# Hedgehog attention and a squared-ReLU FFN: another order of the plan's steps from position 100 on, with its bank, engine, gate and warm-up tables

## The chip, the cores and the metric

The kernel runs on 1 core of one Trainium2 chip. The metric is the device time of one launch in microseconds, taken as the median of the runs. TensorE is called PE (its weight load PEld), VectorE DVE, ScalarE ACT, GpSimd POOL and SyncE SP, as in the profile.

## The reference

Linear attention with learned features over 8 batches, 8 heads, 576 tokens and 64 columns per head, then an FFN over the 4608 rows that the attention gives.

```python
def phi(x):
    proj = np.einsum('bhsd,df->bhsf', x, w_phi)
    proj = proj - np.max(np.abs(proj), axis=-1, keepdims=True)
    return np.concatenate([np.exp(proj), np.exp(-proj)], axis=-1)
q_p, k_p = (phi(q), phi(k))
kv = np.einsum('bhsf,bhsd->bhfd', k_p, v)
z = np.sum(k_p, axis=2)
num = np.einsum('bhsf,bhfd->bhsd', q_p, kv)
den = np.einsum('bhsf,bhf->bhs', q_p, z)[..., None] + 1e-06
x = (num / den).transpose(0, 2, 1, 3).reshape(4608, 512)
h = np.maximum(x @ w_in, 0.0)      # 512 -> 2048
out = h * h @ w_out                # 2048 -> 512
```

`w_phi` is 64x128, so each head has 256 features: exp(proj) and exp(-proj).

## The kernel before, in words

All products are bf16 with f32 sums in PSUM. The work is cut into 8 batches of attention and 9 FFN chunks of 512 tokens: chunk c (0 to 7) takes the first 512 tokens of batch c, and chunk 8 takes the last 64 tokens of each of the eight.

One batch of attention goes through these steps. q, k and v are loaded by POOL's DMA queue (`load`, L254 and L262; `load_q`, L274 and L285). q and k are transposed: from batch 2 on by a DMA transpose that SP issues (`transposed`, L339), before that on PE. PE projects them (L355, with 64 rows of the array; L510 and L577 in the first batch and for the features of q), DVE takes the largest absolute value (`em_ops` L410, `qmax_ops` L517, L389 in the first batch), ACT forms the exponentials (L416 and L398 for k, L592 for q). `v_ops` (L443) multiplies V by exp of its keys' maxima, which ACT wrote (L429, L435); the product stands on DVE or, in batches 0 and 1, on either DVE or POOL. `kv_ops` (L473, L478) sums keys by values in PSUM; ACT or DVE copies the sums to SBUF (L196 on DVE, L198 on ACT). `out_ops` multiplies with the features of q (L607), DVE scales (L619), takes the reciprocal of the denominator (L627) and divides (L631, into the tile xo). xo is transposed to xT (xS for chunk 8): by a DMA transpose on SP (L665), in the first batch on PE with a DVE copy (L656).

An FFN chunk has 16 groups of each kind: `ffn_in` (called F1 here, L751; `ffn_in_small` L762 for chunk 0, by pieces of 128 tokens) multiplies with w_in, `relu_sq` takes the ReLU (L726 on ACT, L728 on DVE, into hr) and the square (L735, on DVE, or in chunks 0 and 1 on either DVE or POOL); `ffn_out` (F2, L816) multiplies with w_out, ACT or DVE copies the sums out (L198, L196), and SP stores them (L832, L835). `last_out` ends chunk 8 by halves of 256 columns (product L780, copies L794 and L796, store L803). The weights are loaded by POOL (`load_win` L301, `load_wout` L307).

None of this is emitted where it is written. Each step is a closure that `Plan.add` records, 1731 in all, and five tables decide the rest. `arrange` (L101) returns the steps in the order of `ORDER`, gives each PSUM group its bank from `BASES`, and reads from `STATES` which of its two engines a step with alternatives takes:

```python
for op in self.ops:
    if op.alt is not None and STATES[op.group] == "1":
        op.eng, op.occ, op.lat = op.alt
for g, b in zip(self.banks, BASES):
    g.base = int(b)
return [self.ops[i] for i in ORDER]
```

`pin` (L139) chains every instruction to the one before it on its engine, so that an engine runs its share of the steps strictly in the order of the table. For the loads it adds a wait for one other step, taken from `GATES`; the last table, `FILL`, puts warm-up matmuls on PE ahead of some steps (L885), which compute nothing that is used:

```python
dep(i, before, mybir.DependencyClass.NoSync)
...
if now[0].seq in GATES:
    dep(i, plan.ops[GATES[now[0].seq]].ins, mybir.DependencyClass.Sync)
```

Of the kernel before, what the change touches and what calls it, by code (L numbers as in the profile page):

```python
# [111 lines left out]
def kernel(  # L112
# [783 lines left out]
    59, 80, 94, 92, 35, 83, 155, 61, 63, 95, 34, 74, 98, 49, 85, 169, 62, 104, 57, 93, 100, 25, 103, 60, 58, 101,  # L896
    158, 102, 84, 81, 99, 97, 127, 143, 105, 24, 82, 106, 96, 159, 107, 125, 28, 128, 108, 129, 126, 156, 160, 131,
    130, 170, 37, 219, 132, 213, 157, 121, 133, 214, 147, 134, 220, 172, 148, 135, 173, 117, 136, 149, 137, 118, 33,
    174, 150, 161, 151, 199, 36, 231, 200, 162, 183, 381, 197, 232, 184, 138, 163, 198, 215, 139, 164, 187, 140, 152,
    165, 188, 322, 216, 189, 374, 166, 323, 325, 185, 153, 217, 167, 154, 221, 168, 233, 222, 337, 326, 218, 38, 331,  # L900
    234, 223, 376, 334, 327, 332, 378, 338, 328, 224, 324, 225, 335, 329, 175, 379, 340, 235, 339, 330, 375, 343,
    171, 333, 236, 176, 352, 226, 341, 336, 344, 342, 177, 377, 190, 353, 178, 346, 179, 370, 186, 246, 191, 261,
    347, 286, 262, 180, 287, 192, 355, 30, 193, 288, 194, 207, 349, 208, 181, 209, 182, 264, 345, 195, 210, 356, 498,
    196, 211, 265, 502, 239, 350, 263, 245, 248, 227, 212, 277, 238, 367, 228, 237, 240, 278, 371, 358, 380, 242,
    229, 247, 372, 364, 244, 357, 254, 253, 230, 241, 39, 243, 506, 256, 373, 368, 255, 249, 32, 369, 257, 348, 250,
    31, 279, 251, 359, 361, 351, 266, 258, 389, 354, 259, 252, 365, 280, 362, 201, 281, 203, 260, 516, 204, 202, 282,
    267, 283, 295, 284, 520, 296, 268, 289, 510, 297, 290, 270, 360, 304, 271, 291, 305, 524, 511, 292, 528, 366,
    293, 269, 272, 306, 388, 298, 363, 307, 299, 552, 529, 308, 205, 300, 206, 577, 556, 301, 302, 386, 309, 313,
    273, 310, 572, 560, 314, 274, 311, 275, 316, 276, 294, 315, 534, 317, 437, 285, 468, 438, 564, 318, 512, 439,
    440, 469, 319, 303, 538, 441, 470, 571, 542, 312, 320, 570, 565, 390, 434, 391, 398, 567, 321, 546, 399, 392,  # L910
    387, 499, 393, 569, 435, 400, 503, 581, 547, 495, 401, 584, 504, 574, 394, 442, 413, 500, 496, 450, 521, 385,
    451, 505, 395, 568, 507, 522, 383, 452, 523, 517, 508, 382, 396, 406, 501, 384, 459, 518, 513, 397, 768, 519,
    585, 535, 497, 460, 514, 539, 536, 436, 515, 411, 461, 407, 531, 767, 540, 446, 402, 532, 415, 549, 573, 509,
    418, 447, 410, 408, 575, 525, 533, 537, 576, 409, 403, 557, 578, 412, 419, 550, 553, 416, 583, 421, 541, 543,
    579, 554, 420, 427, 582, 526, 443, 417, 695, 558, 530, 527, 775, 404, 551, 548, 414, 699, 764, 429, 405, 444,
    765, 424, 422, 771, 426, 425, 555, 544, 561, 766, 423, 545, 471, 428, 769, 562, 453, 703, 559, 580, 454, 477,
    472, 455, 478, 430, 563, 456, 473, 457, 707, 479, 474, 458, 475, 432, 431, 708, 587, 591, 433, 586, 599, 592,
    749, 753, 600, 593, 757, 588, 594, 713, 589, 462, 717, 590, 463, 566, 445, 601, 480, 476, 464, 481, 721, 602,
    465, 709, 466, 482, 725, 448, 609, 483, 467, 484, 486, 603, 487, 595, 604, 761, 485, 726, 780, 449, 488, 731,
    596, 961, 608, 605, 489, 776, 735, 762, 615, 616, 962, 606, 490, 739, 778, 618, 624, 597, 491, 972, 626, 743,  # L920
    610, 623, 492, 607, 970, 617, 598, 692, 493, 777, 744, 631, 625, 494, 640, 967, 693, 656, 704, 641, 657, 773,
    782, 700, 770, 612, 705, 611, 632, 658, 968, 718, 971, 701, 706, 634, 643, 722, 774, 644, 694, 969, 710, 614,
    723, 613, 702, 779, 696, 724, 719, 635, 963, 711, 619, 633, 781, 697, 647, 620, 637, 772, 665, 720, 714, 638,
    666, 965, 621, 966, 698, 667, 629, 715, 728, 646, 636, 639, 716, 648, 712, 674, 729, 740, 622, 642, 630, 730,
    649, 650, 746, 651, 741, 668, 675, 742, 652, 747, 736, 676, 964, 653, 669, 732, 654, 645, 737, 670, 758, 655,
    733, 671, 672, 627, 738, 759, 763, 734, 788, 683, 754, 789, 980, 750, 760, 790, 755, 928, 628, 791, 659, 932,
    660, 751, 756, 677, 684, 661, 892, 783, 662, 685, 678, 936, 748, 663, 679, 752, 896, 680, 681, 800, 796, 784,
    900, 785, 801, 727, 786, 904, 682, 787, 940, 797, 807, 802, 664, 910, 941, 803, 914, 905, 805, 804, 811, 821,
    906, 792, 793, 828, 820, 798, 799, 745, 673, 918, 922, 808, 794, 806, 946, 813, 795, 1162, 829, 950, 840, 831,
    844, 923, 809, 845, 815, 841, 954, 1167, 846, 812, 686, 832, 810, 889, 897, 979, 958, 890, 981, 687, 834, 973,  # L930
    823, 891, 1158, 982, 688, 898, 976, 924, 814, 822, 1164, 893, 833, 959, 983, 1159, 1160, 984, 689, 901, 902, 907,
    1166, 824, 975, 826, 835, 690, 903, 894, 837, 960, 825, 908, 827, 853, 691, 978, 854, 838, 1165, 862, 1170, 855,
    816, 915, 818, 895, 1161, 1163, 830, 856, 911, 899, 817, 916, 1001, 909, 933, 819, 857, 917, 1168, 836, 1004,
    858, 863, 912, 859, 839, 860, 977, 1174, 919, 847, 848, 864, 934, 974, 880, 951, 881, 920, 849, 882, 925, 850,
    935, 913, 929, 926, 952, 865, 843, 851, 937, 842, 930, 871, 866, 1025, 921, 938, 943, 867, 947, 927, 1026, 931,
    872, 939, 944, 852, 868, 1175, 873, 1003, 869, 948, 955, 1176, 861, 874, 997, 875, 956, 998, 1027, 1089, 876,
    877, 878, 1028, 1125, 999, 1129, 985, 1037, 1172, 957, 953, 1000, 1002, 986, 1093, 1097, 949, 987, 945, 988, 870,
    1169, 883, 1101, 1038, 884, 1039, 1042, 1133, 1102, 879, 993, 1040, 885, 994, 886, 1029, 1137, 1005, 1143, 1017,
    887, 1138, 989, 1049, 1094, 1050, 995, 996, 1147, 1095, 1051, 1096, 942, 1018, 1178, 990, 1179, 1086, 1054, 1008,
    1052, 1151, 1020, 1007, 1112, 1010, 1019, 1087, 1180, 991, 1113, 1009, 1006, 1171, 1098, 1090, 1103, 1041, 1155,  # L940
    1181, 992, 1061, 1011, 1099, 1012, 1091, 1156, 1062, 1100, 1073, 1021, 1053, 1023, 1015, 1013, 1063, 1024, 1114,
    1030, 1016, 1022, 1130, 1014, 1031, 1104, 1074, 1088, 1064, 1177, 1032, 1043, 1044, 1075, 1131, 1076, 1105, 1033,
    1116, 1055, 1045, 1122, 888, 1139, 1198, 1034, 1201, 1117, 1065, 1077, 1035, 1106, 1092, 1046, 1047, 1363, 1107,
    1056, 1182, 1194, 1364, 1361, 1057, 1195, 1365, 1111, 1356, 1359, 1115, 1058, 1357, 1059, 1119, 1183, 1196, 1123,
    1067, 1197, 1036, 1124, 1118, 1066, 1358, 1060, 1134, 1068, 1108, 1069, 1120, 1173, 1140, 1200, 1184, 1185, 1152,
    1109, 1070, 1222, 1370, 1366, 1135, 1202, 1071, 1141, 1110, 1078, 1360, 1136, 1223, 1190, 1186, 1079, 1126, 1048,
    1153, 1072, 1224, 1187, 1127, 1154, 1304, 1225, 1188, 1308, 1207, 1286, 1226, 1189, 1205, 1132, 1199, 1148, 1128,
    1295, 1142, 1290, 1191, 1192, 1149, 1355, 1150, 1080, 1203, 1291, 1193, 1081, 1206, 1372, 1294, 1292, 1082, 1144,
    1083, 1209, 1084, 1287, 1145, 1146, 1293, 1312, 1246, 1227, 1296, 1208, 1121, 1247, 1288, 1234, 1204, 1283, 1297,
    1316, 1309, 1298, 1284, 1317, 1248, 1212, 1235, 1322, 1310, 1299, 1236, 1373, 1249, 1313, 1300, 1311, 1213, 1327,  # L950
    1314, 1250, 1157, 1301, 1379, 1328, 1375, 1237, 1285, 1289, 1326, 1376, 1239, 1302, 1380, 1377, 1305, 1323, 1214,
    1362, 1306, 1307, 1303, 1331, 1216, 1378, 1330, 1324, 1341, 1215, 1270, 1238, 1381, 1315, 1382, 1325, 1258, 1334,
    1332, 1217, 1251, 1342, 1210, 1374, 1271, 1398, 1272, 1333, 1211, 1397, 1319, 1218, 1343, 1259, 1085, 1273, 1219,
# [80 lines left out]
```

## Time and profile before

| what | value |
|---|---|
| runs before, median of 3 | 351.43 us (350.83 to 351.53) |
| profiled execution: its own time, and its span | 352.42 us, 350.3 us |
| PE busy | 337.3 us in 3335 instructions |
| DVE busy | 271.6 us in 520 instructions |
| ACT busy | 228.7 us in 432 instructions |
| POOL busy | 96.8 us in 144 instructions |
| moved by DMA | 46.69 MB, mean 133 GB/s |

In the rows of a timeline the first number is the start in us from the span's beginning, the second the length; then come engine, line, operation and tile, output<-input, the shape, and x the number of instructions in the row. Brackets hold the idle time ahead of it on its engine and what ended it. A row of a window holds its limits, its length, the busy us of PE, PEld, DVE, ACT and POOL with their instructions, the granted TensorE clock, the share of the DMA engines, and GB/s.

### The profile page before, as it was taken

How to read it: one execution, taken by the hardware profiler on the slowest of the kernel's cores; microseconds unless marked ns; L12 is line 12 of the kernel's file. 1: busy time of each engine (PE TensorE's matmuls, PEld its weight loads, DVE VectorE, ACT ScalarE, POOL GpSimd, SP SyncE). 2: the span in 40 equal slices, each digit the busy share in tenths (PEclk: the TensorE clock that was granted, in tenths of full speed). 3: DMA queues.
4: the chain of work that ended last, by engine and by line, in shares of the span. 5: the costliest groups of instructions: out<-in, count | busy, mean ns of one | idle time of the engine just before them, and what ended most of it. 6: DMA issues, size and time to landing. Idle time of an engine off the chain costs nothing.

```text
span 350.3 us, 8403 instructions
## 1 busy us (share of the span) xinstructions
PE 337.3 (96%) x3335; PEld 191.7 (55%) x3370; DVE 271.6 (78%) x520; ACT 228.7 (65%) x432; POOL 96.8 (28%) x144
## 2 busy tenths in 40 slices
PE   8889999999999999999999989999999999999994
PEld 5669976544654555465546544465455544444451
DVE  4999998899979988898889988789697923745030
ACT  4999897599779775987999684784766111233111
POOL 8735450397518600283100460010000000000000
PEclk9999999999999999999999999999999999999998
DMA  8999989799999997899999999778954521001016
GB/s 100 183 201 202 196 98 144 154 127 156 192 184 134 155 148 150 189 153 117 136 190 164 141 155 165 169 116 144 207 110 77 117 87 67 32 0 60 2 37 173
DMA packets 124327, 46.69 MB, mean 133 GB/s; under 512 B 92800, under 2 KB 119808, under 8 KB 124288
## 3 DMA queue, kind: packets, MB, share of 16 engines
q0 software_dynamic: 45216, 18.36, 46.9%
q1 hardware_dynamic: 78752, 27.50, 39.7%
q8 instruction: 26, 0.43, 0.5%
q10 hardware_dynamic: 320, 0.30, 0.4%
q14 instruction: 13, 0.11, 0.1%
HBM read 36.77 MB, written 9.44 MB: 132 GB/s over the span
## 4 chain that ended last, share of the span: by engine, by line
PE 84%; ACT 5%; DVE 4%; DMA 3%; issue 2%; DVEq 0%; ACTq 0%; POOLq 0%
PE psum L816 32%; PE psum L751 30%; PE psum L607 5%; PE psum L355 5%; PE psum L473 4%; PE psum L762 3%; DMA xT<-xo 2%; DVE va L443 2%; ACT qf L592 2%; PE psum L577 2%; PE psum L780 1%; DMA xk<-in_k_dram 1%; PE psum L478 1%; ACT kp L398 1%; DVE mq L517 1%
## 5 line engine op out<-in xcount | busy, mean ns | idle before, releaser
L816 PE MATMUL psum<-wout,h 128*128 128x512 bf16 x525 | 129.4, 379 | 2.6 <-issue 1.1
L751 PE MATMUL psum<-xT,win 128*128 128x512 bf16 x448 | 107.6, 379 | 1.2 <-DMA xT<-xo 1.2
L726 ACT ACTIVATE hr<-psum 128x512 bf16<-128x512 f32 x99 | 57.1, 596 | 63.4 <-PE psum L751 48.0
L816 PEld LDWEIGHTS <-h 128*128 128x128 bf16 x560 | 51.3, 98 | 55.9 <-issue 0.8
L751 PEld LDWEIGHTS <-win 128*128 128x128 bf16 x512 | 46.9, 98 | 53.6 <-issue 1.9
L735 DVE TENSOR_TENSOR h<-hr 128x512 bf16<-128x512 bf16 x143 | 56.3, 417 | 14.8 <-ACT hr L726 14.2
L592 ACT ACTIVATE qf<-psum 128x1024 bf16<-128x1024 f32 (+1 forms) x50 | 45.8, 945 | 7.6 <-PE psum L577 7.3
L517 DVE TENSOR_REDUCE mq<-psum 128x8 f32<-128x1024 f32 (+1 forms) x40 | 44.1, 1108 | 2.3 <-PE psum L355 1.1
L728 DVE TENSOR_SCALAR hr<-psum 128x512 bf16<-128x512 f32 x45 | 30.5, 686 | 18.8 <-PE psum L751 17.9
L410 DVE TENSOR_REDUCE mk<-psum 128x8 f32<-128x1024 f32 (+1 forms) x35 | 38.1, 1112 | 5.5 <-PE psum L355 4.7
L416 ACT ACTIVATE kp<-psum 128x1024 bf16<-128x1024 f32 (+1 forms) x35 | 32.7, 937 | 14.1 <-DVE mk L410 14.0
L607 PEld LDWEIGHTS <-qf 128*128 128x128 bf16 x640 | 28.2, 97 | 13.1 <-issue 0.9
L619 DVE TENSOR_TENSOR psum<-psum,en 128x520 f32<-128x520 f32 (+1 forms) x40 | 27.7, 699 | 8.7 <-PE psum L607 6.7
L416 ACT ACTIVATE kn<-psum 128x1024 bf16<-128x1024 f32 (+1 forms) x35 | 32.7, 937 | 0.0
L607 PE MATMUL psum<-kv,qf 128*128 128x65 bf16 x640 | 31.2, 193 | 0.1
L443 DVE TENSOR_TENSOR va<-xv,va 64x256 bf16<-64x256 bf16 (+2 forms) x68 | 30.2, 459 | 0.8
L254 POOL DMA_DIRECT2D xv<-in_v_dram x26 | 19.2, 751 | 34.0 <-ACT va L435 8.9
L631 DVE TENSOR_TENSOR xo<-psum,rden 128x512 bf16<-128x512 f32 (+1 forms) x40 | 27.3, 684 | 0.7
L274 POOL DMA_DIRECT2D xq<-in_q_dram x24 | 17.2, 720 | 35.7 <-ACT va L435 13.9
L254 POOL DMA_DIRECT2D xk<-in_k_dram x28 | 20.5, 736 | 12.4 <-ACT va L429 5.2
L473 PE MATMUL psum<-va,kp 128*128 128x65 bf16 x256 | 19.5, 193 | 0.8 <-DVE va L443 0.4
L473 PE MATMUL psum<-va,kn 128*128 128x65 bf16 x256 | 19.5, 193 | 0.0
(68 smaller groups left out, 368.4 us busy)
## 6 DMA issues: line engine op xcount, KB each, us to landing
out_dram<-ot SPq DMA_DIRECT2D x32, 256.0 KB, 2.8
xk<-in_k_dram POOLq DMA_DIRECT2D x26, 128.0 KB, 4.6
xq<-in_q_dram POOLq DMA_DIRECT2D x24, 128.0 KB, 5.8
xv<-in_v_dram POOLq DMA_DIRECT2D x24, 128.0 KB, 5.0
win<-in_moe_w_in_dram POOLq DMA_DIRECT2D x4, 512.0 KB, 11.7
wout<-in_moe_w_out_dram POOLq DMA_DIRECT2D x4, 512.0 KB, 11.7
xq<-in_q_dram POOLq DMA_DIRECT2D x4, 256.0 KB, 6.3
xv<-in_v_dram POOLq DMA_DIRECT2D x2, 512.0 KB, 9.3
```

The source lines that it names most:

```text
L254: pin(nc.gpsimd.dma_start(out=x[:, a * 512 : z * 512].rearrange("p (h x) -> p h x", x=4 * D), in_=src[b][2 * a : 2 * z, 0:512, :].rearrang ...
L410: pin(nc.vector.tensor_reduce(out=mk_view(g), in_=ps2(pj)[:, :, : n * Fd].rearrange("p e (i f) -> p e i f", f=Fd), axis=AX.X, op=ALU.max, ...
L416: pin(nc.scalar.activation(out=dst[slot][:, :, :n, :].rearrange("p e i f -> p e (i f)"), in_=ps2(pj)[:, :, : n * Fd], func=ACT.Exp, scale= ...
L443: pin(engine().tensor_tensor(out=t[:, :, :D].rearrange("p m (x c) -> p m x c", c=2), in0=x.rearrange("p (m x c) -> p m x c", m=n, c=2), in ...
L473: pin(nc.tensor.matmul(out=o[:, sg, hi, :], lhsT=(kp, kn)[sg][kgroup[pr]][:, j % 2, 2 * hi + j // 2, :], rhs=va[s2][sg][:, 8 * pr + 4 * hi ...
L517: pin(nc.vector.tensor_reduce(out=mqb[:, c, :, :n], in_=ps2(pj)[:, :, : n * Fd].rearrange("p e (i f) -> p e i f", f=Fd), axis=AX.X, op=ALU ...
L592: pin(nc.scalar.activation(out=o, in_=i_, func=ACT.Exp, scale=sgn))
L607: pin(nc.tensor.matmul(out=o[:, u // 4, u % 4 * D1 : (u % 4 + 1) * D1], lhsT=(qp, qn)[sg][slot][:, u * m : u * m + P], rhs=kv_sb[s2][:, h ...
L726: pin(nc.scalar.activation(out=hr[sl], in_=ps1(g), func=ACT.Relu))
L735: pin(engine().tensor_tensor(out=dst, in0=i_, in1=i_, op=ALU.mult))
L751: pin(nc.tensor.matmul(out=o, lhsT=win[mc // 4][:, kc, mc % 4 * P : (mc % 4 + 1) * P], rhs=x, start=(kc == 0), stop=(kc == KC - 1)))
L816: pin(nc.tensor.matmul(out=ps1(g), lhsT=h2[c % 2][mc // 4][:, mc % 4, tt * P : (tt + 1) * P], rhs=wout[mc // 4][:, mc % 4, :], start=(mc = ...
```

## The change

The steps, their closures and all shapes stay as they are. The five tables are replaced. `ORDER` is the same up to position 99 and a different order of the same steps from position 100 on; every PSUM group may have another bank; 135 of the 275 digits of `STATES` differ; nearly all `GATES` name other steps; five entries of `FILL` change, and the warm-up matmuls go from 76 to 79. A line or two of each:

```diff
 ORDER
-    59, 80, 94, 92, 35, 83, 155, 61, 63, 95, 34, 74, 98, 49, 85, 169, 62, 104, 57, 93, 100, 25, 103, 60, 58, 101,
+    59, 80, 94, 92, 35, 83, 155, 61, 63, 95, 34, 74, 98, 49, 85, 169, 62, 104, 106, 101, 81, 57, 60, 96, 84, 93, 121,
 GATES (load: the step that it waits for)
-    370: 220, 372: 116, 764: 57, 765: 500
+    370: 223, 372: 239, 764: 592, 765: 417
 FILL (step: bank, matmuls, column)
-    158: (7, 5, 0), 127: (2, 2, 0), 149: (6, 1, 0), 161: (6, 5, 0),
+    158: (7, 11, 0), 135: (3, 2, 0), 149: (3, 1, 0), 187: (2, 2, 0),
```

By engine, what `STATES` moves: squares on POOL 1 before and 18 after (DVE 143 and 126), V products on POOL 0 and 3, ReLUs on ACT 99 and 91 (DVE 45 and 53), copies of kv on ACT 17 and 21 (DVE 15 and 11), copies of FFN outputs on ACT 21 and 18 (DVE 14 and 17).

The first place is POOL's queue in the ramp, from the last small loads of batch 1's first half to the weight loads. Names ending in 0 or 1 before the underscore are the two buffers (even and odd batches). Before:

```order
L262 DMA xk1_75<-in_k_dram 64x4x64
L262 DMA xv1_79<-in_v_dram 64x4x64 x2
L301 DMA win3_65<-in_moe_w_in_dram 128x4x512
L301 DMA win2_64<-in_moe_w_in_dram 128x4x512
L262 DMA xk1_75<-in_k_dram 64x4x64
L307 DMA wout1_67<-in_moe_w_out_dram 128x4x512
L254 DMA xv1_79<-in_v_dram 128x8x256
```

And after the change:

```order
L262 DMA xk1_75<-in_k_dram 64x4x64
L262 DMA xv1_79<-in_v_dram 64x4x64 x2
L443 TENSOR_TENSOR va00_98<-xv0_78,va00_98 128x8x64 x3
L301 DMA win2_64<-in_moe_w_in_dram 128x4x512
L301 DMA win3_65<-in_moe_w_in_dram 128x4x512
L262 DMA xk1_75<-in_k_dram 64x4x64
L285 DMA xq1_77<-in_q_dram 128x8x128
L254 DMA xv1_79<-in_v_dram 128x8x256
```

Three V products of batch 0 (va00) now stand on POOL ahead of two w_in loads, and a load of q has come ahead of one of V.

The second place is POOL's queue where the loads of batch 3 (buffers xk1, xq1, xv1) and the squares of chunk 1 (tiles h21) meet. Before:

```order
L254 DMA xv0_78<-in_v_dram 128x2x256 x3
L262 DMA xk0_74<-in_k_dram 64x4x64
L735 TENSOR_TENSOR h21_1_137<-hr0_128 128x512
L254 DMA xk0_74<-in_k_dram 128x2x256
L274 DMA xq1_77<-in_q_dram 128x2x256 x3
L262 DMA xq1_77<-in_q_dram 64x4x64
L262 DMA xv1_79<-in_v_dram 64x4x64
```

And after:

```order
L735 TENSOR_TENSOR h21_2_138<-hr0_128 128x512
L254 DMA xk0_74<-in_k_dram 128x2x256
L735 TENSOR_TENSOR h21_2_138<-hr2_130 128x512
L274 DMA xq1_77<-in_q_dram 128x2x256
L735 TENSOR_TENSOR h21_3_139<-hr0_128 128x512
L262 DMA xv1_79<-in_v_dram 64x4x64
L735 TENSOR_TENSOR h21_3_139<-hr3_131 128x512
L262 DMA xq1_77<-in_q_dram 64x4x64 x2
```

Squares now stand between the loads, and the last two loads of q for batch 3 stand behind one.

The third place is SP's queue where batch 6's results (xo) are transposed for FFN chunk 6 (xT00 and xT01 are its two tiles), between the transposes of q and k (qT, qf) and the stores of FFN outputs (ot). Before:

```order
L339 DMA_TRANSPOSE qT1_83<-xq1_77 128x18x128
L665 DMA_TRANSPOSE xS_127<-xo4_117 128x4x64
L544 DMA_TRANSPOSE qf0_110<-xq0_76 128x16x128
L665 DMA_TRANSPOSE xT00_123<-xo2_115 128x4x128
L835 DMA out_0_dram<-ot2_142 128x512
L541 DMA_TRANSPOSE qf1_111<-xk0_74 128x4x128 x2
L665 DMA_TRANSPOSE xT01_124<-xo1_114 128x4x128
L835 DMA out_0_dram<-ot0_140 128x512
L665 DMA_TRANSPOSE xT01_124<-xo3_116 128x4x128
L835 DMA out_0_dram<-ot2_142 128x512
L665 DMA_TRANSPOSE xT00_123<-xo0_113 128x4x128
```

And after:

```order
L339 DMA_TRANSPOSE qT1_83<-xq1_77 128x18x128
L544 DMA_TRANSPOSE qf0_110<-xq0_76 128x16x128
L541 DMA_TRANSPOSE qf1_111<-xk0_74 128x4x128 x2
L665 DMA_TRANSPOSE xS_127<-xo4_117 128x4x64
L835 DMA out_0_dram<-ot1_141 128x512
L835 DMA out_0_dram<-ot0_140 128x512
L665 DMA_TRANSPOSE xT01_124<-xo1_114 128x4x128
L665 DMA_TRANSPOSE xT00_123<-xo0_113 128x4x128
L665 DMA_TRANSPOSE xT00_123<-xo2_115 128x4x128
L665 DMA_TRANSPOSE xT01_124<-xo3_116 128x4x128
```

The four transposes of a chunk now follow one another without stores between them, and two stores stand ahead of them. At the end of the program SP's stores of 64-row and of half-width outputs change places so that the last one is that of a half (L803) where it was a 64x512 one (L832), and PE's last groups are halves (L780) where they were whole (L816).

More of the change, by code (lines that the diff above doesn't have):

```diff
@@ L895 @@
     51, 75, 123, 86, 52, 87, 50, 53, 124, 76, 115, 88, 54, 116, 55, 77, 89, 90, 22, 113, 79, 78, 23, 56, 114, 91, 27,
[80 rows of a table removed]
[80 rows of a table added]
 ]
 BASES = (
-    '7762205543351613247724322302602306674447442731320126074760270660422244446264622606176160063720462403'
-    '6376440226246040224115440556605777123504024764140002202442402462567677750767766755002420370621246244'
-    '6422641733061210160110014062624510460664262260150054644505457100420626040500266266201520104005412405'
-    '4450466203010042644646455323343013201315330627045322761544210720376027202404120456561523'
+    '7762205543351613247224130267600006014426144423372722432066476322205400002466447767060714652527026264'
+    '4514066626606022362400143014120450355526006432000060633066626644345442252241355555626036457000004226'
+    '0262000474263544524454555420066575400242024245445777646456676676702400060102440042225667223277631721'
+    '7662400045554222200220276157475446776616744061610750065317541133205611015076263435756203'
 )
 STATES = (
-    '0000000000000000010100110100110100010010000010000010000000000000100000001000100010100111000000001000'
-    '0010000000001010000000100010000101011110000010001000001001001011001000110100000001001100001010001101'
-    '100001100010011100101010011010110011101001101010100000011101001000010000010'
+    '0000010001010000000010011110011100010000011101101000010100000101000110011000110100111100110010110001'
+    '0011110000110000100000001100000100011000000111000000010000110011110010000100000010101011110010110001'
+    '011111001001100000000000100001001010011110011110101011101001010010101111001'
 )
 GATES = {
[11 rows of a table removed]
[11 rows of a table added]
 }
@@ L1002 @@
     40: (0, 15, 0), 42: (0, 3, 0), 64: (0, 4, 0), 66: (0, 6, 0), 109: (0, 3, 0), 144: (0, 6, 0), 53: (0, 5, 0),
-    77: (3, 2, 0), 155: (7, 19, 0), 158: (7, 5, 0), 127: (2, 2, 0), 149: (6, 1, 0), 161: (6, 5, 0),
+    77: (3, 2, 0), 155: (7, 19, 0), 158: (7, 11, 0), 135: (3, 2, 0), 149: (3, 1, 0), 187: (2, 2, 0),
 }
```

180 rows, old and new, of tables (GATES, ORDER) are left out of this document.

## The prediction

> **What bounds the kernel.** I read the page's totals first, then its windows, then the waits and the chain of waits, and last the timelines of the places that the new tables touch.
>
> ```profile
> span 350.3 us, 8403 instructions
> PE 337.3 (96%) x3335; PEld 191.7 (55%) x3370; DVE 271.6 (78%) x520; ACT 228.7 (65%) x432; POOL 96.8 (28%) x144
> PE   8889999999999999999999989999999999999994
> ...
> DVE  4999998899979988898889988789697923745030
> ```
>
> TensorE is busy for 96% of the span, and VectorE is the next engine with 78%. The change adds three warm-up matmuls to PE and takes nothing from it; the product work is the same. What it can win or lose is PE's idle and badly used time, and that is concentrated, as the windows show (columns: busy us and instructions of each engine, granted clock, DMA share, GB/s):
>
> ```profile
> 10.00:20.00 10.00, 8.34 (x104) 6.03 (x101) 9.81 (x22) 9.96 (x28) 7.24 (x10) 1.00 1.56 189
> 20.00:30.00 10.00, 9.22 (x190) 7.94 (x188) 9.93 (x22) 9.44 (x21) 5.00 (x7) 1.00 1.33 201
> 200.00:210.00 10.00, 8.77 (x65) 4.05 (x63) 8.71 (x18) 9.10 (x15) 6.56 (x11) 1.00 1.53 160
> 340.00:350.30 10.30, 5.63 (x33) 2.89 (x30) 0.69 (x1) 1.58 (x3) 0.00 (x0) 0.87 0.56 154
> ```
>
> From 10 to 30 us DVE and ACT are full and PE waits for them: this is the ramp, and part of PE's busy time there is warm-up matmuls. Around 205 us PE loses 1.2 of 10 us, and at the end it drains; the granted clock is 1.00 until then. Elsewhere the page's PE row has a 9. The waits name what is left in between (engine, line, releaser: us, count, mean):
>
> ```profile
> PEld L355 <- issue: 11.0, 26, 0.4
> ...
> PE psum L751 <- DMA xT<-xo: 1.2, 1, 1.2
> ...
> PE psum L473 <- DVE va L443: 0.4, 1, 0.4
> ```
>
> The first row is the switch into the projections of q and k (half-array products). Each entry costs about 0.4 us in any order. I counted the stretches in the new order that interrupt the full-array products: a few more entries, fewer with a wait behind them; I cost this at nothing. The other two are true waits, and small. So the sum consists of the ramp, two waits for transposes, and the tail; against them stands what new work on POOL does.
>
> **The ramp.** Positions 0 to 99 are unchanged, so the program agrees up to about 17 us. These are its next rows on DVE, ACT and PE (start, length), the length of a kv group of 16 products from the chain of waits, and the one length of an element-wise product on POOL:
>
> ```profile
> 17.75 3.75 DVE L443 TENSOR_TENSOR va<-xv,va 128x512 bf16<-128x512 bf16 x11
> 21.43 0.41 DVE L196 CAST kv<-psum 128x260 bf16<-128x260 f32 x1
> ...
> 22.10 2.34 DVE L517 TENSOR_REDUCE mq<-psum 128x8 f32<-128x1024 f32 x2
> 24.36 1.29 DVE L619 TENSOR_TENSOR psum<-psum,en 128x520 f32<-128x520 f32 x2
> ```
>
> ```profile
> 17.83 0.53 ACT L435 ACTIVATE va<-mk 128x16 bf16<-128x16 f32 x4
> ...
> 20.74 1.02 ACT L592 ACTIVATE qf<-psum 128x1024 bf16<-128x1024 f32 x1
> 21.64 0.39 ACT L198 ACTIVATE kv<-psum 128x260 bf16<-128x260 f32 x1
> ```
>
> ```profile
> 29.13 1.06 PE L762 MATMUL psum<-xT,win 128*128 128x128 bf16 x16
> ```
>
> ```profile
> 50.15 0.64 PE psum L473 x16
> ```
>
> ```profile
> L735 POOL TENSOR_TENSOR h<-hr x1: 1039/1039/1039, 80.2 to 80.2; 128x512 bf16<-128x512 bf16 x1
> ```
>
> Three of the twelve V products (L443) leave DVE for POOL. DVE gains 3 x 3.75/11 = 1.0 us. On POOL no V product was ever timed; the nearest row is the square of the same 128x512 shape, 1.04 us, and I take that. The three follow one another: from about 18.4 (the first exps at 17.83 + 0.53) they end at about 18.4 + 3 x 1.04 + a tenth or so between them = 21.7, where DVE ended all twelve at 22.1. The kv groups (L473) of those heads follow, and the last kv copy stands on ACT behind an exp of 1.02 (L592) whose projection stands on PE behind that same group: 21.7 + 0.64 + 1.02 + 0.39 = 23.75, with about 0.75 for that projection and the hand-overs 24.5 for the first L607, and 0.4 for its two groups (the L607 row below) 24.9 for the first scaling (L619), against 24.36. Thus DVE's relief isn't passed on: **+0.6**. The bounds: if DVE's end decides alone, 1.0 is won, and 0.3 more behind it (in DVE's rows up to the third key maximum of the next batch, four squares at 0.417 fewer, one ReLU, a qT and a small copy more), so -1.3; if a V product on POOL takes twice the square's 1.04, +0.6 + 3.1 = +3.7. The term is then seen at the first L762, which I expect at 29.6 instead of 29.13. The win loads stand behind the V products on POOL, but their bytes stand in a full DMA queue (189 to 201 GB/s in the windows) and land in time.
>
> **POOL beside DVE.** The squares on POOL go from 1 to 18. On DVE they cost:
>
> ```profile
> L735 DVE TENSOR_TENSOR h<-hr 128x512 bf16<-128x512 bf16 x143 | 56.3, 417 | 14.8 <-ACT hr L726 14.2
> ...
> L443 DVE TENSOR_TENSOR va<-xv,va 64x256 bf16<-64x256 bf16 (+2 forms) x68 | 30.2, 459 | 0.8
> ```
>
> ```profile
> 79.39 1.29 DVE L728 TENSOR_SCALAR hr<-psum 128x512 bf16<-128x512 f32 x2
> ```
>
> DVE gets 17 x 0.417 = 7.1 us freer. The one square on POOL (80.17 to 81.21) ran beside this row and the key maximum after it, which read PSUM; no row shows a POOL product beside a DVE instruction with both inputs in SBUF, so its cost is bounded. From below it is nothing (POOL's descriptor work does not lengthen DVE's squares). From above each would be held for the whole length of the other: 3 x 1.04 = 3.1 in the ramp, where DVE is full, and for the squares 17 x 1.04 x (56.3 + 30.2)/350 = 4.4 us of DVE, of which half arrives at PE (13 of the first 25 slices of DVE's row have a 9), 2.2. I take **+1.0**, about one POOL instruction, nearer to nothing because most of the squares lie where DVE has other work from PSUM.
>
> The Trainium skill bears on this, in "SBUF — State Buffer", section "Who interferes with whom": a DVE instruction with two SBUF inputs contends with a GpSimd instruction that reads SBUF, and whichever comes first holds the shared ports for its whole length while the other is blocked. By that rule the upper end would hold instead of my one microsecond; no row here shows it either way, and it is the lock among the rivals.
>
> **Waits for transposes.** These are the rows of the wait at 206.6:
>
> ```profile
> 199.63 0.41 PE L607 MATMUL psum<-kv,qf 128*128 128x65 bf16 x8
> ...
> 208.58 0.61 PE L751 MATMUL psum<-xT,win 128*128 128x512 bf16 x2 [1.18 <-DMA xT<-xo]
> ```
>
> ```profile
> xT<-xo SPq DMA_TRANSPOSE x28, 3.1
> ```
>
> ```profile
> 201.65 6.88 DMA xT<-xo
> ...
> 209.18 0.86 PE psum L816 x4
> ```
>
> From the last L607 of a batch to the first L751 that reads its transposed rows, the path took 8.9 us here, because the transpose, 3.1 us in the median of the DMA view, took 6.88 among the twelve loads issued around it. One batch on it took:
>
> ```profile
> 245.43 0.41 PE L607 MATMUL psum<-kv,qf 128*128 128x65 bf16 x8
> ...
> 252.60 0.59 PE L751 MATMUL psum<-xT,win 128*128 128x512 bf16 x2
> ```
>
> ```profile
> 246.84 1.21 SPq L665 DMA_TRANSPOSE xT<-xo  x1
> ...
> 248.74 1.29 SPq L665 DMA_TRANSPOSE xT<-xo  x1
> ```
>
> ```profile
> DMA to landing us min/median/max: 3.1/3.4/3.7
> ```
>
> so 1.4 to the issue of the third transpose and up to 3.7 more, 4.5 to 5.1 us; the fourth stood behind a store, was issued at 248.74 and landed just ahead of the L751 at 252.60, under 7 us of cover. The new order has no store between the four. The new order puts between those two points, in chunk 5, 28 products at 0.86/4 = 0.215 us and 16 projections, 7.2 to 7.6 us, and in chunk 6 only 20 products and 16 projections, about 5.9 with the switches; the other chunks have 6.3 or more. The loads near chunk 5 are gated on the same xo; near chunk 6 four xv loads are issued with the last transpose. I take 0.2 and 0.6 of waits in place of 1.18: **-0.4** (bounds: -1.2, no wait at all; +3.1, if chunk 6 meets an 8.9 us path and chunk 5 one of 8.9).
>
> The transposes of q for batch 3 are the other kind:
>
> ```profile
> xq<-in_q_dram POOLq DMA_DIRECT2D x16, 32.0 KB, 6.5
> ...
> qT<-xq SPq DMA_TRANSPOSE x6, 6.4
> ```
>
> ```profile
> 16.73 0.64 POOL L262 DMA_DIRECT2D xv<-in_v_dram  x1
> ```
>
> The last two q loads now stand on POOL behind a square of chunk 1. From that square's F1 product it takes about 1 (ReLU) + 1.04 + 2 x 0.64 + 6.5 + 6.4 = 16.2 us to the transposed q, and PE has 14 groups x 0.86 + 4.5 = 16.5 us of work before it needs it. Level: **+0.3** (0 to 2, two POOL instructions late).
>
> **The tail.**
>
> ```profile
> 345.67 0.60 ACT L198 ACTIVATE ot<-psum 128x512 f32<-128x512 f32 x1 [0.84 <-PE psum L816]
> ...
> 346.71 0.54 SPq L832 DMA_DIRECT2D out_dram<-ot  x1
> ```
>
> ```profile
> 339.18 0.42 DVE L794 COPY otl<-psum 128x256 f32<-128x256 f32 x1 [2.01 <-PE psum L780]
> ```
>
> The old program ends with a 512-column copy and a store that stands behind another on SP; the new one ends with three half groups (L780), a 0.42 us copy, and its store alone on SP: 0.2 for the copy and 0.2 of the queue, **-0.4** (-0.6 to 0).
>
> **Sum.** +0.6 + 1.0 - 0.4 + 0.3 - 0.4 = +1.1. The profiled execution took 352.42 us, 0.99 above the median of the runs, 351.43. So it would become 353.5, and the runs **352.5**.
>
> **Rivals.** *DVE relief* (faster): the ramp is DVE's, 8.1 us of products leave it, nothing blocks, and DVE's end decides. Place: the first L619; it decides if POOL's third V product ends before about 21. Price: -1.3 in the ramp, the V wait of 0.4 gone, port 0, the rest as above: -1.3 - 0.4 + 0.3 - 0.4 - 0.4 = -2.2, **349.2**; with no transpose wait left 348.1. For it: DVE at 9.81 and 9.93 of 10. Against: ACT is as full, and the kv copies are ACT's.
> *The lock* (slower): the upper end of the port, 3.1 + 2.2 in place of 1.0, gives **356.8**. For it: V products on both engines at the same microsecond. Against: most DVE rows read PSUM.
> *No effect*: PE's 96% stays, each wait is replaced by one as long: **351.4**.
>
> **Numbers.** Forecast (351 to 354.2) 0.41, of which 0.28 slower, 0.09 same, 0.04 faster; relief 0.32 (0.31 faster, 0.01 same); lock 0.17, slower; no effect 0.10 (0.02, 0.05, 0.03). With 0.2% (0.70 us), about what a measurement of this kernel can tell from no change: faster 0.37, same 0.15, slower 0.48. The range takes in relief with all waits gone, 348.1 less half a microsecond, and the lock: 347.6 to 357.0. It also holds the ramp's and the transposes' upper ends, 1.1 + 3.1 and 1.1 + 3.5 above the median.
>
> **What would show it.** The profile after should have the first L762 at 29.6, L443 on POOL at about 1.04 us and DVE's L443 still at 0.34; twice that on either side is the lock. A wait of L751 for xT should stand in chunk 6, not at chunk 5. The first L762 before 28.7 is relief. Wrong altogether would be a new wait above 1 us elsewhere, or PE's projections costing more entries than before: "L355 <- issue" well above 11.0.

## The result: 8.2 us slower, and the profile after

The changed kernel takes 359.69 us (median of four runs, 359.45 to 360.56) against 351.48 us of before: a ratio of 1.0226, 95% interval 1.0207 to 1.0246. The forecast was 352.5 with a range up to 357.0, so the direction was right and the size far off: +8.2 us where +1.1 was summed, beyond even the dearest rival, 356.8.

The page after (profiled execution 360.56 us):

```profile
span 358.8 us, 8421 instructions
...
PE 342.6 (95%) x3338; PEld 194.4 (54%) x3373; DVE 277.7 (77%) x507; ACT 225.5 (63%) x425; POOL 119.0 (33%) x164
...
PE   7879999999899999999999999999989999999995
...
PEclk9978999999999999999999999999999999999999
```

Two things are to be seen. 17 squares and three V products were taken from DVE, and yet it is busy for 277.7 us where it had 271.6. And the granted clock, full throughout the first slices of before, has a 7 and an 8 in the third and fourth slice. The windows show the place (busy us of PE, PEld, DVE, ACT, POOL; then the granted clock):

```profile
10.00:20.00 10.00, 8.80 (x114) 6.78 (x112) 9.98 (x19) 9.48 (x27) 6.79 (x9) 1.00 1.54 184
20.00:30.00 10.00, 7.92 (x104) 5.90 (x104) 7.39 (x13) 5.20 (x11) 8.72 (x10) 0.66 1.22 183
30.00:40.00 10.00, 9.78 (x183) 8.71 (x182) 9.85 (x20) 8.87 (x17) 3.90 (x5) 1.00 1.22 139
```

To find where the 8 us come from, I added up for each trace the length of PE's product work in PE's own order, and read off how much later than before the same amount of it is reached (worked out from the starts of PE's weight loads; us later than before; e2 to e10 are the experiments below):

| product work done | changed | e2 | e3 | e5 | e6 | e10 |
|---|---|---|---|---|---|---|
| 5 us | 0.4 | -0.4 | 0.0 | -0.4 | -0.1 | -0.2 |
| 10 us (about 25 us of time before) | 5.0 | 2.5 | 1.4 | 2.5 | 1.3 | 1.2 |
| 25 us | 6.3 | 3.3 | 2.2 | 3.7 | 2.5 | 2.5 |
| 65 us | 6.6 | 4.6 | 3.5 | 4.1 | 2.7 | 2.6 |
| 75 us | 8.6 | 5.6 | 4.5 | 6.1 | 4.7 | 3.9 |
| 180 us | 8.6 | 5.5 | 4.4 | 7.2 | 4.7 | 4.2 |
| 185 us (chunk 5's transpose) | 7.4 | 4.3 | 3.2 | 6.0 | 3.5 | 3.0 |
| 220 us | 7.5 | 4.5 | 3.4 | 6.2 | 3.6 | 3.2 |
| 230 us (chunk 6's transpose) | 9.0 | 5.7 | 5.1 | 6.4 | 3.8 | 3.3 |
| 317 us, all | 9.0 | 5.7 | 5.1 | 6.4 | 3.8 | 3.3 |

More than half of the loss is in the ramp, 2 us lie between 65 and 75, the two transposes cancel, and the tail gives 0.5 back (9.0 at the last product, 8.5 in the span). These are the ramp's rows after, DVE first, then POOL, then PE's first FFN product:

```profile
18.16 5.47 DVE L443 TENSOR_TENSOR va<-xv,va 128x512 bf16<-128x512 bf16 x9
23.66 2.35 DVE L517 TENSOR_REDUCE mq<-psum 128x8 f32<-128x1024 f32 x2
...
29.14 1.31 DVE L619 TENSOR_TENSOR psum<-psum,en 128x520 f32<-128x520 f32 x2 [1.98 <-issue]
```

```profile
18.54 1.05 POOL L443 TENSOR_TENSOR va<-xv,va 128x512 bf16<-128x512 bf16 x1 [1.31 <-ACT va L435]
20.01 2.85 POOL L443 TENSOR_TENSOR va<-xv,va 128x512 bf16<-128x512 bf16 x2 [0.41 <-ACT va L435]
```

```profile
33.47 1.07 PE L762 MATMUL psum<-xT,win 128*128 128x128 bf16 x16
```

DVE needs 5.47 us for nine V products where before eleven took 3.75: beside POOL's three it is stopped. POOL's own are stopped too, 2.85 us for two. The first scaling comes at 29.14 (forecast 24.9) and the first L762 at 33.47 (forecast 29.6). The same is seen where a square on POOL lies beside a product on DVE. First DVE, then POOL, around 40 and 96 us:

```profile
40.45 1.21 DVE L735 TENSOR_TENSOR h<-hr 128x512 bf16<-128x512 bf16 x1
```

```profile
40.30 1.06 POOL L735 TENSOR_TENSOR h<-hr 128x512 bf16<-128x512 bf16 x1
```

```profile
96.60 1.98 DVE L443 TENSOR_TENSOR va<-xv,va 128x1024 bf16<-128x1024 bf16 x1
```

```profile
96.97 1.05 POOL L735 TENSOR_TENSOR h<-hr 128x512 bf16<-128x512 bf16 x1
```

A square of 0.42 us takes 1.21 and ends at 41.66, 0.3 us behind POOL's; a V product of 0.7 us takes 1.98, although it began 0.37 us ahead of the square on POOL, which kept its 1.05. I went through all DVE instructions that overlap a product on POOL: reductions, ReLUs, copies, the scalings and the divides, which have at most one input in SBUF, keep their lengths (L619 700 ns in both kernels, L410 1216 against 1218 before); only V products and squares stretch, squares by 2.1 us in all and V products by 4.4. Then PE runs dry from 20 us on and its clock is cut:

```profile
22.00:23.00 1.00, 0.61 (x15) 0.51 (x15) 1.00 (x1) 0.16 (x1) 1.00 (x2) 0.90 1.23 203
23.00:24.00 1.00, 0.59 (x7) 0.42 (x7) 0.92 (x4) 0.01 (x1) 1.00 (x2) 0.50 1.51 157
...
28.00:29.00 1.00, 1.00 (x13) 0.58 (x12) 0.00 (x0) 0.05 (x1) 1.00 (x2) 0.50 1.25 204
```

By the trace's record of the clock PE works at half its clock from 22.79 to 29.62 us, though it is busy again from 24. The Trainium skill, "TensorE: Matmul & The Clock Gate", section "What's actually happening", says that the array falls to half its clock after an idle window of about 3.4 us and needs a busy one to come back. The trace agrees with the half, but here the window was far from empty: in the 3.41 us ahead of the cut PE was busy for 1.91. The full clock came back 6.83 us after the cut.

### The profile page after: what moved, and what is told of

The parts are those of the page before. It is cut to its first block, busy times and chain, and to the rows that moved or that the text cites. A ratio compares the mean times of both kernels' runs of the same rounds, so it can differ in the third digit from the quotient of the medians.

```text
span 358.8 us, 8421 instructions
## 1 busy us (share of the span) xinstructions
PE 342.6 (95%) x3338; PEld 194.4 (54%) x3373; DVE 277.7 (77%) x507; ACT 225.5 (63%) x425; POOL 119.0 (33%) x164
## 4 chain that ended last, share of the span: by engine, by line
PE 84%; DVE 7%; issue 3%; DMA 3%; ACT 1%; SPq 0%; POOL 0%; DVEq 0%; ACTq 0%; POOLq 0%
PE psum L816 31%; PE psum L751 29%; PE psum L607 6%; PE psum L473 5%; PE psum L355 5%; PE psum L762 3%; DMA xq<-in_q_dram 2%; PE psum L577 2%; DVE va L443 2%; DMA xT<-xo 1%; PE psum L478 1%; DVE mk L389 1%; PE psum L780 1%; DVE mq L517 1%; DVE hr L728 1%
## 5 line engine op out<-in xcount | busy, mean ns | idle before, releaser
L816 PE MATMUL psum<-wout,h 128*128 128x512 bf16 x525 | 129.1, 379 | 2.2 <-issue 0.6
L751 PE MATMUL psum<-xT,win 128*128 128x512 bf16 x448 | 108.0, 379 | 2.0 <-DMA xT<-xo 1.2
L726 ACT ACTIVATE hr<-psum 128x512 bf16<-128x512 f32 x91 | 53.1, 597 | 60.5 <-PE psum L751 38.4
L816 PEld LDWEIGHTS <-h 128*128 128x128 bf16 x560 | 51.1, 98 | 54.7 <-issue 0.2
L751 PEld LDWEIGHTS <-win 128*128 128x128 bf16 x512 | 47.1, 98 | 53.5 <-issue 3.2
L735 DVE TENSOR_TENSOR h<-hr 128x512 bf16<-128x512 bf16 x126 | 51.4, 432 | 19.2 <-ACT hr L726 18.7
L410 DVE TENSOR_REDUCE mk<-psum 128x8 f32<-128x1024 f32 (+1 forms) x35 | 38.4, 1110 | 7.7 <-PE psum L355 7.4
L728 DVE TENSOR_SCALAR hr<-psum 128x512 bf16<-128x512 f32 x53 | 35.8, 684 | 9.7 <-PE psum L751 8.6
L619 DVE TENSOR_TENSOR psum<-psum,en 128x520 f32<-128x520 f32 (+1 forms) x40 | 27.6, 700 | 9.2 <-PE psum L607 5.7
L443 DVE TENSOR_TENSOR va<-xv,va 64x256 bf16<-64x256 bf16 (+2 forms) x65 | 34.3, 546 | 0.5
L198 ACT ACTIVATE ot<-psum 128x512 f32<-128x512 f32 x18 | 10.7, 595 | 21.9 <-PE psum L816 21.8
L735 POOL TENSOR_TENSOR h<-hr 128x512 bf16<-128x512 bf16 x18 | 19.4, 1081 | 11.3 <-ACT hr L726 9.2
```

Source lines behind the costliest of these rows:

```text
L410: pin(nc.vector.tensor_reduce(out=mk_view(g), in_=ps2(pj)[:, :, : n * Fd].rearrange("p e (i f) -> p e i f", f=Fd), axis=AX.X, op=ALU.max, ...
L443: pin(engine().tensor_tensor(out=t[:, :, :D].rearrange("p m (x c) -> p m x c", c=2), in0=x.rearrange("p (m x c) -> p m x c", m=n, c=2), in ...
L726: pin(nc.scalar.activation(out=hr[sl], in_=ps1(g), func=ACT.Relu))
L728: pin(nc.vector.tensor_scalar(out=hr[sl], in0=ps1(g), scalar1=0.0, scalar2=None, op0=ALU.max))
L735: pin(engine().tensor_tensor(out=dst, in0=i_, in1=i_, op=ALU.mult))
L751: pin(nc.tensor.matmul(out=o, lhsT=win[mc // 4][:, kc, mc % 4 * P : (mc % 4 + 1) * P], rhs=x, start=(kc == 0), stop=(kc == KC - 1)))
```

## The experiments

**e1: V products back.** The three digits of `STATES` for them; nothing else.

```diff
-    '0000010001010000000010011110...
+    '0000000000000000000010011110...
```

> The changed kernel with only the three V products of batch 0 back on DVE; order, banks, gates and squares stay. Lock theory (a POOL product with SBUF inputs and a DVE product with two SBUF inputs stop each other, PE then runs dry and its clock is cut): the ramp's loss of about 5.0 us is this, so about 355 us; DVE's V products are back at 0.34 us each in a row, the granted clock stays at 1.00 from 20 to 30 us. Rival, the order itself (kv copies behind exponentials on ACT, other steps ahead on DVE) is late in the ramp: within 1 us of the changed kernel's 359.7.

Measured: 356.45 us, ratio 1.0151 (1.0104 to 1.0198). The trace's ramp loss falls from 5.0 to 1.1 us and the clock stays at 1.00. The hold theory stands for the ramp; the interval is wide, and 4 us are left that it doesn't explain.

**e2: squares back, V products still on POOL.** Eighteen digits of `STATES`.

> The changed kernel with only the 18 squares on POOL put back on DVE; the three V products stay on POOL. Lock theory: PE's losses of 1.3 us around 41 to 48 us and 1.9 us around 93 to 99 us come from products held up beside squares on POOL; DVE gets 18 x 0.416 = 7.5 us more work but loses about 5 us of holds, so 357 to 358.5 us, and no DVE square above 0.45 us. Rival, DVE as the bound (the relief by POOL was real): slower than 359.7, about 361 us.

Measured: 358.41 us, the median of three runs (357.27 to 362.49), ratio 1.0209 (1.0137 to 1.0281); a fourth run, left out of both, took 365.44. The times follow the mean clock (357.27 us at 1.000, 358.41 at 0.995, 362.49 at 0.991, 365.44 at 0.984) and scatter too far to tell this kernel from the changed one. Its trace (357.27 us) is worth more. The three V products stop DVE just as in the changed kernel, but in this execution the clock was not cut:

```profile
17.33 5.47 DVE L443 TENSOR_TENSOR va<-xv,va 128x512 bf16<-128x512 bf16 x9
```

```profile
20.00:30.00 10.00, 7.49 (x141) 5.67 (x140) 8.94 (x18) 6.68 (x12) 8.66 (x11) 1.00 1.33 192
```

and the ramp loses 2.5 us, not 5.0. So the hold reaches PE with about 1.1 us (2.5 against 1.4 in e3), and the clock makes 2.5 of the 5.0 in the profiled execution of the changed kernel.

Why the clock was spared here is not shown, but the traces point at when the steps of the clock fall. The cut of the changed kernel lasted 6.83 us and that of e4 half of it, 3.41 (24.18 to 27.60). Each began a whole number of steps of 3.41 us after the first mark of the clock's record (5 steps after 5.72 us, 6 after 3.70). In the step ahead of the cut PE was busy for 1.91 us in the changed kernel and for 1.29 in e4. In e2 the first mark is at 4.54, and the idle time falls into two steps, with 2.08 and 2.12 us of busy PE.

**e3: all products on DVE.** Both edits.

> The changed kernel with the three V products and the 18 squares all on DVE. Lock theory: nearly all of the 8.2 us comes back; the wait for the transpose in chunk 6 (1.2 us) stays and stands against the one that went in chunk 5 (1.2) and the shorter tail (0.5): 351 to 353 us. Rival, the order itself: above 355 us.

Measured: 357.61 us, ratio 1.016 (1.0121 to 1.0198). Here the rival came true: with no product on POOL at all the new order is still 5.6 us slower by the medians, and 5.1 us later at the trace's last product. My theory was the smaller part of the cause: it explains 2.6 of the 8.2 us by the medians, and 3.9 of 9.0 in the traces. V products are as fast as before, twelve in a row, but the first scaling is 1.1 us later than the 24.36 of before, and the bracket names its wait, a tile that ACT gives late:

```profile
17.72 4.02 DVE L443 TENSOR_TENSOR va<-xv,va 128x512 bf16<-128x512 bf16 x12
...
25.50 1.31 DVE L619 TENSOR_TENSOR psum<-psum,en 128x520 f32<-128x520 f32 x2 [0.85 <-ACT en L551]
```

What is called the order here is all that is left of the change: besides `ORDER` the banks, the gates, the fillers and the other 114 digits of `STATES`. No run parts them.

**e4: the old order with the three V products on POOL.**

```diff
-    '0000000000000000010100110100...
+    '0000010001010000010100110100...
```

> The kernel before with one thing of the change: the same three V products on POOL, in the old order. Lock theory: DVE's nine V products are stretched as in the changed kernel, the kv groups come 1.5 to 3 us late, the clock is cut: 353.5 to 356.5 us. Rival, the order itself is late: 351 to 352 us, since three products leave a full DVE.

Measured: 355.75 us, ratio 1.0105 (1.0089 to 1.0122), 3.7 us for three digits, and 3.0 of the 3.2 us that its trace is late at the end are there at 10 us of product work; the mean granted clock was 0.989 to 0.993 in its four runs, 0.996 to 1.000 in those of before. The hold needs nothing of the new order.

**e5: the idle PE filled.**

```diff
 FILL = {
+    131: (3, 22, 0),
```

> The changed kernel with 22 more warm-up matmuls (2.3 us) ahead of the first kv group that waits for a V product, where PE stood idle and the granted clock then fell to 0.50; nothing else. Clock theory (part of the ramp's 5.0 us is the clock that an idle PE is granted, not the hold itself): the clock stays at 1.00 from 22 to 30 us, the profiled ramp loses 2.5 instead of 5.0 us, about 357.5 to 358.5 us. Rival, the hold alone: the same 359.7 or a little more, since the filler only stands in PE's way.

Measured: 358.04 us, ratio 1.0163 (1.0148 to 1.0178), 1.65 us less than the changed kernel by adding 2.3 us of useless work. DVE is held as long as ever; only the clock is whole:

```profile
17.34 5.47 DVE L443 TENSOR_TENSOR va<-xv,va 128x512 bf16<-128x512 bf16 x9
```

```profile
20.00:30.00 10.00, 9.35 (x162) 7.72 (x161) 8.94 (x18) 6.68 (x12) 7.90 (x10) 1.00 1.32 190
```

All four runs have a mean clock of 1.000 (the changed kernel's 0.988 and 0.995). The clock's part is shown. It is 2.5 us in the profiled execution and some 1.6 in the median.

**e6: an earlier gate for four loads,** on top of e1.

```diff
-    1368: 1267,
+    1368: 1209,
```

> The kernel of the first experiment (three V products on DVE) with one gate changed: the four loads of v that were issued beside the last transpose of chunk 6 wait for an earlier step (about 20 us earlier). Theory, these loads stretch that transpose: its 4.3 us become about 3, the wait of 1.1 us of L751 goes, 1 us faster than that kernel (356.45 to about 355.4). Rival, the distance of 20 products is too short by itself: the wait stays above 0.8 us.

Measured: 355.33 us, ratio 1.0088 (1.0073 to 1.0103), 1.1 us less than e1. In the changed kernel these rows show the loads beside chunk 6's last transpose, then the chain of waits there, and the landing times of the four transposes:

```profile
257.44 2.84 POOL L254 DMA_DIRECT2D xv<-in_v_dram  x4 [20.68 <-DVE xo L631]
```

```profile
257.56 4.53 DMA xT<-xo
...
262.13 1.89 PE psum L751 x8
```

```profile
DMA to landing us min/median/max: 2.3/2.4/4.5
```

In e6 the last of the four loads is issued at 242.49, the four transposes take 2.4 us at most, and L751 doesn't wait:

```profile
242.49 0.70 POOL L254 DMA_DIRECT2D xv<-in_v_dram  x1 [6.55 <-DVE rden L627]
```

```profile
DMA to landing us min/median/max: 2.3/2.4/2.4
```

20 products of cover were enough; the loads were the cause.

**e7: seven more entries into the half array,** in the old order: a neighbouring projection moved behind the FFN group that followed it, seven times after 100 us.

```diff
 ORDER, each of seven places
-    Pk, Pq, F2
+    Pk, F2, Pq
```

> The kernel before with seven pairs of neighbouring half-array projections (L355) pulled apart by one full-array FFN group each; same instructions, only seven more entries into and exits from the half array, all after 100 us. Theory, entries and exits are not free: by the old trace 44 stretches cost 10.98 + 6.73 - 1.73 us, 0.36 each, so +2.5 us, about 354.5 us. Rival, they are hidden or cost as little as I took in the sum: within 0.5 us of before.

Measured: 355.29 us, ratio 1.0088 (1.0071 to 1.0104), +3.3 us. The row of these entries among the waits grows by exactly seven (before: 11.0 in 26):

```profile
PEld L355 <- issue: 14.0, 33, 0.5
```

In the trace five of the places cost a clean 0.21 us each in lateness; the others brought waits with them, since a projection that comes later makes what hangs on it later (0.9 us of a kv group for a ReLU, 0.7 us of L751 for another). Entries are not free, and a net 0.21 us is the price of one with its exit. The Trainium skill, "TensorEngine Tiling (Array Packing)", section "Tiling Modes", says that changing the tiling mode drains the array; the 0.21 us fits that, though no view shows the drain itself.

**e8: writes alone beside DVE.** The old order; POOL writes the places of the three V products three times each and reads nothing.

```diff
+    for _ in range(3):
+        pin(nc.gpsimd.memset(t[:, 8 * g0 : 8 * g1, :D], 0.5))
```

> The kernel before in the old order, where POOL does not multiply the three V products of batch 0 but only writes their places, three times each (this part of the values is left out of the result): POOL is busy beside DVE's V products and reads nothing from SBUF. Theory, only a POOL instruction that reads SBUF holds a DVE instruction with two SBUF inputs: DVE's V products keep 0.34 us each in a row and the time is 350.5 to 352 us. Rival, any POOL instruction beside them holds them: as with the products, above 354 us.

Measured: 352.53 us, ratio 1.0015 (1.0003 to 1.0028). POOL first, then DVE:

```profile
17.56 3.38 POOL L462 MEMSET va<- 128x512 bf16 x6
```

```profile
17.53 2.75 DVE L443 TENSOR_TENSOR va<-xv,va 128x512 bf16<-128x512 bf16 x8
```

Eight V products take 0.34 us each beside six writes that cover them from end to end. The time is 0.5 us above what the theory expected, but far below the rival's. It is the reading that holds: the Trainium skill, "SBUF — State Buffer", section "Who interferes with whom", says so, and the traces agree. They don't show that the first to start wins, as the V product at 96.60 us in the changed kernel had begun before the square that held it.

**e9: the wait of before taken away.** In the old order seven loads of the twelve around chunk 5's stretched transpose now stand behind the FFN group that reads it.

```diff
 GATES
-    1363: 1117
+    1363: 1295
 ORDER: 1363, 1364, 1361, 1365, 1366, 1173, 1370 behind 1355
```

> The kernel before with one thing moved: seven of the twelve loads that were issued around its stretched transpose of chunk 5 (five of q, two of v, needed 20 us later and more) stand behind the first FFN group that reads that transpose. Theory, loads beside it stretch the transpose from about 3 to 6.9 us and PE waits 1.18 us for it: the wait goes and about 1 us with it, 0.997 of the time before. Rival, the transpose is late for another reason (the divide, SP): within 0.3 us of before.

Measured: 351.09 us against 352.16 of before, ratio 0.9971 (0.9953 to 0.9990). It is faster than both kernels: the transposes land within 4.0 us, and the wait of 1.18 us is gone from PE's list.

```profile
DMA to landing us min/median/max: 2.4/3.3/4.0
```

**e10: e6 with the last three squares of POOL back on DVE.** Three digits of `STATES`.

> The kernel with three V products on DVE and the earlier gate, with the last three squares of POOL (93 to 98 us) back on DVE, where DVE's V product of 1024 columns took 1.98 us instead of 0.69 and PE waited behind it. Lock theory: about 0.7 to 1 us faster than that kernel, 354.4 us. Rival, DVE is full there and the squares delay the same work: no faster than 355.3.

Measured: 354.69 us, ratio 1.0059 (1.0037 to 1.0081), 0.6 us less than e6 by the medians. The V product that took 1.98 us in the changed kernel:

```profile
92.91 0.68 DVE L443 TENSOR_TENSOR va<-xv,va 128x1024 bf16<-128x1024 bf16 x1
```

**e11: e6 with all 18 squares on DVE.**

> The same kernel with all 18 squares on DVE. If the holds beside squares cost more than the 7.5 us of DVE work that they take away, as the term of 2.2 us at the upper end would have it: 353 to 354 us. If both about cancel, as the first and third experiment's traces show (4.67 against 5.06 us behind the kernel before): 355 to 356 us.

Measured: 355.7 us, ratio 1.0091 (1.0057 to 1.0126), no different from e6. Relief and holds cancel over the whole of the squares, within what these intervals can tell.

**e12: the old order with 18 more squares on POOL.** The edit gives POOL all 18 squares that the change has there; with the one of before they are 19.

> The kernel before in its old order with the 17 other squares on POOL too, which the change puts there. Relief theory: DVE is 7.1 us freer, faster than before by up to 1 us. Lock theory: each square on POOL beside a DVE product with two SBUF inputs holds it, and the loads behind the squares are issued up to a microsecond later: 0.5 to 3 us slower, 1.0015 to 1.008.

Measured: 362.46 us, ratio 1.0292 (1.0256 to 1.0329): 10.3 us, over three times the dearer of the two expectations, and both theories missed it. A square on POOL stands in one queue with the loads that POOL issues. In an order not laid out for that, it comes late, and the four buffers of hr run out. DVE's ReLUs, then PE's products, wait for POOL:

```profile
82.86 0.69 DVE L728 TENSOR_SCALAR hr<-psum 128x512 bf16<-128x512 f32 x1 [0.87 <-POOL h L735]
86.21 1.29 DVE L728 TENSOR_SCALAR hr<-psum 128x512 bf16<-128x512 f32 x2 [2.65 <-POOL h L735]
```

```profile
PE psum L816 <- POOL h L735: 3.3, 2, 2.4
```

The holds on DVE beside squares are of the same size as in the changed kernel, about 5 us in both traces. The same 18 squares cost 10.3 us here and nothing that the runs can tell in e6 against e11, so the price of a POOL square depends on its place in POOL's queue first. PE's own wait for POOL is 3.3 us of the 10.3; the rest was not split.

## Why the prediction was wrong, step by step

**The ramp, "+0.6", and POOL beside DVE, "+1.0": the steps that failed most.** Together 1.6 was summed for ramp and holds; the ramp alone lost 5.0 us in the profiled execution. Three parts make it: the order of steps 1.4 (e3), the hold 1.1 (e2 against e3), the cut clock 2.5 (e5). That the +0.6 (0.5 by its own terms, 24.9 against 24.36) had the sign of the first is luck: its path ran through POOL's V products, and e3, which has none, is late by another wait, that for `en`. The hold itself lay between my bounds and below the lock's 3.1. What I didn't have, in the sum or in a rival, is what comes behind a hold: PE idles for 2 us in a stretch in which it has nothing else to do, and the idle is paid a second time by the clock. I had quoted the granted clock of 1.00 and read it as given. The argument for taking the low end, that the squares lie beside PSUM work, was of no use for the V products, which on both engines read SBUF at the same microsecond; the rival named that and had only 0.17.

**"I cost this at nothing": the entries into the half array.** The waits of the changed kernel have these two rows:

```profile
PEld L355 <- issue: 9.8, 23, 0.4
...
PEld L577 <- issue: 6.6, 17, 0.7
```

and of before, beside the 11.0 in 26 for L355:

```profile
PEld L577 <- issue: 3.6, 9, 0.8
```

L355 alone, the row that I had named as the sign, fell. The entries moved to the other half-array product, L577, from 9 to 17; both rows together went from 14.6 us in 35 to 16.4 in 40. Counting also those without such an idle time, the new order has 61 entries in all where the old has 55; at the 0.21 us of e7 six of them are 1.3 us, an estimate that no run of the new order tested. I had counted more entries in the order and set them against waits that I expected to be fewer; nothing in the profile supported that.

**"Waits for transposes, -0.4": right places, half of the mechanism.** Chunk 5's wait went (1.2 us won, at its lower bound), and chunk 6's took its place with 1.2 instead of 0.6. e6 and e9 show that the loads beside a transpose decide both. The distance that I counted decides neither: with the loads gone, chunk 6's 20 products are enough.

**The q transposes, "+0.3".** No wait of that kind is in the trace after; the products of q's projection for batch 3 run on. The level sum came out on the good side.

**PE's waits elsewhere** had no term in the sum and so stood in it at nothing, which failed: 1.3 us were lost between 10 and 25 us of product work and 2.0 between 65 and 75. Part of it is holds (the rows around 40 and 96 us above; e10 shows 0.4 to 0.8 for the second place). Another part is DVE's own order, in which a kv copy that PE needs stands behind other work. This row of e3, which has no holds, shows it in the second place:

```profile
92.15 0.41 PE L607 MATMUL psum<-kv,qf 128*128 128x65 bf16 x8 [0.58 <-DVE kv L196]
```

It was not tested by itself.

**The tail, "-0.4".** Measured -0.5. The last copy is the short one and its store goes at once:

```profile
354.63 0.42 DVE L794 COPY otl<-psum 128x256 f32<-128x256 f32 x1 [0.62 <-PE psum L780]
```

In ratios the 2.26% are: 0.63 the clock (e5), 0.75 the rest of the V products' hold and the gate (e6), 0.29 three squares (e10), and 0.59 of order, entries among it. The last is the remainder of e10 and was split no further by a run. The table does not let the entries be most of it: e10 loses 1.2 us in the ramp, 1.3 between 10 and 25 us of work and 1.3 between 65 and 75, where by my count of the trace the two stretches hold one entry more each and the ramp none, and only 0.3 between 75 and 180, which holds two more. The intervals of e6 and e10 overlap, so the 0.29 rests on its trace as much as on its time.

## What to carry to other kernels

Before an element-wise product is given to GpSimd to relieve VectorE, look at what VectorE runs in that microsecond: here two products with both inputs in SBUF took turns, and what was a relief of 1.0 us for DVE on paper stretched its other nine products by 2.4 us. Where PE gets its input just in time, price an idle stretch with what the clock does after it, and keep filler ready there. And in an order searched by a planner, count what the planner doesn't see, here changes of array mode and loads beside a transpose, and give each its measured price before calling it equal.

## What the runs showed of the hardware

In these traces a GpSimd product with inputs in SBUF stops VectorE products with two SBUF inputs until it ends (0.42 us became 1.21, 0.7 became 1.98, in the last case though VectorE had begun first) and is stopped by them (1.05 us became up to 1.77); a GpSimd write of the same shape stops nothing (0.34 us each, e8). After 3.41 us in which TensorE was busy for 1.91 the granted clock was 0.50 for 6.83 us in the profiled execution of the changed kernel, and in e2's profile, with the same hold on VectorE, not at all: the cut varies from run to run, and with it the time of such a kernel (357.27 to 365.44 us in e2). Four loads of 128 KB issued beside a transpose made it 4.5 us instead of 2.4.
